# Softmax groups of one batch from batch 4 on, in an FFT filter with a soft mixture of experts

## The chip, the core and the metric

The kernel runs on one core of a Trainium2 chip. The metric is the device time of one launch in microseconds (us), the median of several runs. The layouts of inputs and outputs on the host are not timed.

## What is computed

x has 8 batches of 2496 rows and 256 columns. Each column is filtered in the frequency domain, and the filtered rows, all 19968 of them, go through a soft mixture of 8 experts with 4 slots each.

```python
y = irfft(rfft(x, axis=1) * (filt_r + 1j * filt_i), n=2496, axis=1)   # per batch
x = y.reshape(8 * 2496, 256)
logits = x @ phi                                   # (19968, 32)
d = exp(logits - logits.max(0)); d /= d.sum(0)     # softmax over all rows: dispatch
slot_input = d.T @ x                               # (32, 256), then each expert's MLP:
slot_out = relu(slot_input[e] @ w1[e]) @ w2[e]     # 4 slots for each e
c = exp(logits - logits.max(1)); c /= c.sum(1)     # softmax over the 32 slots: combine
out = c @ slot_out
```

The softmax over all rows is taken in groups of batches, with a running maximum and running sums, as in online softmax.

## The kernel before, in words

The inverse transform is never made for y: by linearity the logits and the slot inputs are formed from the filtered spectra, and only logits and weights are transformed.

A batch goes through these steps. `s1_unit(b, u)`, 11 for each batch, splits x into a high part `xh` (ScalarE, ACT) and a low part `xl` (GpSimd, POOL), multiplies both by a small DFT (three matmuls, L308), and writes the result `at` to DRAM. `x_unit(b, c)`, 10 for each batch, loads it in another order (`ash`), does the second DFT (L339), and multiplies by the filter on VectorE (DVE; L352, L353, L355) with help from POOL (L355, L356). `t_unit(b, c)`, 10 for each batch, transposes the product (L366) into a spectra tile `y_b_c`, copied out by ACT (L368); every second one also makes logits (`l`, L377, copied to `lt`). A spectra tile is kept until its group has used it, in `ypool`, a ring of `YB` buffers of 2 KB for each partition.

When the last batch of a group has its spectra, `chain(g)` runs. In order, by tile names: `ltr` (transposes of `lt`, copied by DVE to `lsb`), `v1` (L423, copied by ACT, L430), `v` (transposes, L443, copied by DVE), `lg` (logits in sequence order, L450; DVE takes maxima into `cm`, `cmax`), `mt` and `mb` (the maximum turned and spread, with `mx` and `dg` on DVE between them), `m_run` (the new running maximum, which needs that of the group before), `d` (subtract on DVE, exp on ACT, L489), `u` (L506, copied by ACT, L516), `u2` (transposes, L523, copied by DVE), `dt` (L537, copied by ACT), `dd` (transposes, L553, copied by DVE), `z` and `s` (L561, L581: the sums over the group's spectra tiles, which are free after it), and `s_run`, the running sum. The combine softmax of the same logits (`rm`, L602 to L610, exp L605) goes on beside it. A chain of a pair has 128 rows where one of a single batch has 64; the tiles `cc` (lsb, u2), `ca` (v1, u, dt) and `cb` (v, d, dd) have one buffer each, so a chain in the pool `work` begins when the one before has let go of them. The last chain has tiles of its own, in the pool `late`, and four PSUM banks; the others share two.

A chain is a generator; after each slot of the main loop the oldest one is moved on by two steps. The instructions so recorded are then put in order by a scheduler, which plans each engine's order by times of its own; on the chip each engine takes its instructions strictly in that order. What waits for what is therefore fixed when the program is built.

After the last batch the expert weights, 64 tiles of 256 KB on SyncE's (SP's) DMA queue, go into whatever is free: five tiles in `late`, then the oldest spectra buffers, then the buffers of the finished steps, and at the end the spectra buffers of the last two batches. Then come `psi`, the experts (`h` L816, `o` L833), and the output: for each batch in `OUT_ORDER`, matmuls (L903), copies into `ob` tiles of 1 MB (L912), and their DMAs.

The names that the change touches:

```python
GROUPS = ((0, 1), (2, 3), (4, 5), (6,), (7,))       # chain(g) for each
YB = 34                                             # buffers of spectra tiles
load_ws(ypool, "y", YB - 2 * CPB)                   # weights into the oldest 14 of them
obp_cm, obp = open_pool("obp", 6, "right")          # output tiles
```

Of the kernel before, what the change touches and what calls it, by code (L numbers as in the profile page):

```python
# [35 lines left out]
THIRDS = ((20, 0), (20, 1), (20, 2), (21, 0))  # L36
NE, SPE, FF = 8, 4, 1024
SLOTS = NE * SPE
GROUPS = ((0, 1), (2, 3), (4, 5), (6,), (7,))
NG = len(GROUPS)  # L40
NSPILL = 2
OUT_ORDER = (4, 5, 0, 1, 2, 3, 6, 7)
# [13 lines left out]
WM = 3  # L56
MV = 4
PA = 6
YB = 34
WL = 5  # L60
SB = 3

# [157 lines left out]
def fft_soft_moe(ctx, tc, x, fr, fi, fny, phi, w1, w2, cst, w1q, bmat, out):  # L220
# [35 lines left out]
    def open_pool(name, bufs, side):  # L256
        cm = tc.tile_pool(name=name, bufs=bufs, side=side, reuse_waits="tile")
        return cm, cm.__enter__()

    lgp_cm, lgp = open_pool("lgp", 1, "left")  # L260
    ypool_cm, ypool = open_pool("ypool", YB, "left")
    x0_cm, x0p = open_pool("x0p", 6, "left")
# [127 lines left out]
    def chain(g):  # L390
        bs = GROUPS[g]
        wk = late_pool[0] if g == NG - 1 else work
# [315 lines left out]
    assert next(ash_next, None) is None and next(b_next, None) is None  # L708
    last = {bs[-1]: g for g, bs in enumerate(GROUPS)}
    active = []  # L710
# [10 lines left out]
    def hop_slot(n):  # L721
        for _ in range(HOPS):
            hop()
# [18 lines left out]
    def load_ws(pool, tag, n, each=1, bufs=None):  # L742
        for _ in range(n):
            if len(wt) == len(order):
                return
            t = pool.tile([P, each * 512], F32, tag=tag, name=f"w_{len(wt)}", bufs=bufs)
            for k in range(min(each, len(order) - len(wt))):
                load_w(t[:, k * 512 : (k + 1) * 512])

    last_s1 = max(at_slot)  # L750
    for n in range(NS + LT):
# [25 lines left out]
        hop_slot(n)  # L777
    load_ws(ypool, "y", YB - 2 * CPB)
    load_ws(prod, "ash", ASH, bufs=ASH)
# [9 lines left out]

    load_ws(ypool, "y", YB)  # L790
    work_cm.__exit__(None, None, None)
    tail_cm, tail = open_pool("tail", 2, "left")
    for g in range(NSPILL):
        lgs[g] = tail.tile([KR, NH, len(GROUPS[g]), 2, SLOTS], F32, tag="cl", name=f"cl_{g}", bufs=NSPILL)
        sp.dma_start(lgs[g], c_dram[g])
# [52 lines left out]
    late_cm.__exit__(None, None, None)  # L848
    prod_cm.__exit__(None, None, None)
    tabs_cm.__exit__(None, None, None)  # L850
    obp_cm, obp = open_pool("obp", 6, "right")

    outs = [(ps_x, "x"), (ps_c, "c"), (ps_s1, "s1")]
    nout = [0]
    where = {b: (g, b2) for g, bs in enumerate(GROUPS) for b2, b in enumerate(bs)}

# [5 lines left out]
    def combine(b, st):  # L862

        g, b2 = where[b]
        nb = len(GROUPS[g])
        cl = lgs[g]
# [96 lines left out]
```

## Time and profile before

| what | value |
|---|---|
| median of 3 runs | 427.81 us (427.04 to 427.97) |
| profiled execution, whole | 425.78 us |
| its span, first to last instruction | 423.9 us |
| TensorE (PE) busy | 374.5 us, 88% |
| DVE, ACT, POOL busy | 269.8, 218.6, 201.9 us |
| moved by DMA | 107.07 MB, mean 253 GB/s |
| mean granted TensorE clock | 0.944 |

The durations below come from one profiled execution; 1.9 us of its time lie outside its span. Names in profile rows have lost their numbers and their digits: `s` on L308 is `s1`, `s` on L581 is the sum, `v` on L423 is `v1`, `u` on L523 is `u2`. Each fp32 matmul counts as two instructions on most lines. A row of the timeline has start, duration, engine and line; the distance from one row's start to the next is what a piece takes of PE, since matmuls overlap.

### The profile page before, as it was taken

What the parts mean: (1) busy time and instruction counts of PE and PEld (TensorE: products, weight loads), DVE (VectorE), ACT (ScalarE), POOL (GpSimd) and SP (SyncE); (2) the same over time, 40 slices, a digit from 0 to 9 for tenths busy, and PEclk for the clock granted to TensorE, in tenths of its full rate; (3) what the DMA queues carried; (4) which work ended last, traced back from release to release, by engine and by line L of the source; (5) the groups of instructions that cost most, each with busy time, mean ns of one, the idle gap of its engine ahead of it and who ended that gap; (6) DMA issues with size and microseconds to landing.
All of it is one profiled execution on the core that took longest, in us unless ns stands there. A gap on an engine that the chain in (4) does not pass through costs nothing.

```text
span 423.9 us, 12672 instructions
## 1 busy us (share of the span) xinstructions
PE 374.5 (88%) x5065; PEld 291.3 (69%) x5065; DVE 269.8 (64%) x496; ACT 218.6 (52%) x475; POOL 201.9 (48%) x234
## 2 busy tenths in 40 slices
PE   7557998999999999999989999989998799999740
PEld 2225876788877787886867688778767435898730
DVE  1341764886989955878998387896378322787330
ACT  2465666676677656765792333461446121675320
POOL 0027778797768655965966056572200401750000
PEclk9688999999999999999999999999998999999555
DMA  8999999999889686978996524333199895699994
GB/s 209 238 306 288 331 321 327 334 294 344 246 262 337 213 264 206 289 214 256 269 280 167 186 82 121 101 103 101 55 344 347 268 275 185 249 394 381 386 362 166
DMA packets 61820, 107.07 MB, mean 253 GB/s; under 512 B 6142, under 2 KB 37758, under 8 KB 60226
## 3 DMA queue, kind: packets, MB, share of 16 engines
q1 hardware_dynamic: 61762, 106.26, 79.3%
q8 instruction: 40, 0.66, 0.6%
q14 instruction: 18, 0.15, 0.1%
HBM read 63.50 MB, written 42.74 MB: 251 GB/s over the span
## 4 chain that ended last, share of the span: by engine, by line
PE 61%; DMA 16%; DVE 12%; ACT 3%; issue 2%; SPq 2%; POOL 0%; ACTq 0%; DVEq 0%
PE x L339 15%; PE s L308 8%; PE t L366 6%; DMA out<-obr 6%; DMA xt<-in_x 6%; PE s L581 4%; PE l L377 4%; PE out L903 3%; PE v L423 3%; PE dt L537 2%; DMA ash<-a_dram 2%; DVE t L353 2%; PE o L833 2%; PE lg L450 2%; PE s L305 2%
## 5 line engine op out<-in xcount | busy, mean ns | idle before, releaser
L295 POOL TENSOR_TENSOR xl<-xt,xh 117x512 fp32r<-117x512 f32 x77 | 103.0, 1350 | 52.7 <-ACT xh L294 49.9
L339 PE MATMUL x<-b_t,ash 128*128 128x128 f32 x640 | 91.5, 284 | 6.1 <-DMA ash<-a_dram 3.1
L339 PEld LDWEIGHTS x<-b_t,ash 128*128 128x128 f32 x640 | 81.2, 194 | 17.0 <-issue 5.0
L356 POOL TENSOR_TENSOR yt<-yt,t 128x256 f32<-128x256 f32 x80 | 65.9, 826 | 40.7 <-DVE t L353 30.5
L352 DVE TENSOR_TENSOR yt<-x,fr_t 128x512 f32<-128x512 f32 x80 | 54.7, 684 | 39.9 <-PE x L339 36.9
L294 ACT CAST xh<-xt 117x512 fp32r<-117x512 f32 x77 | 46.8, 622 | 35.4 <-DMA xt<-in_x 12.1
L368 ACT COPY y<-t 128x512 f32<-128x512 f32 x80 | 46.5, 591 | 34.3 <-PE t L366 28.6
L312 ACT COPY at<-s 120x512 f32<-120x512 f32 x83 | 48.4, 587 | 21.7 <-PE s L305 8.6
L353 DVE TENSOR_TENSOR t<-x,fi_t 128x512 f32<-128x512 f32 x80 | 54.3, 678 | 0.0
L366 PE MATMUL t<-cst_t,yt 128*128 128x128 f32 x320 | 48.5, 276 | 0.7 <-POOL yt L356 0.4
L355 DVE TENSOR_TENSOR yt<-yt,t 128x256 f32<-128x256 f32 x60 | 43.3, 730 | 0.8
L366 PEld LDWEIGHTS t<-cst_t,yt 128*128 128x128 f32 x320 | 37.3, 141 | 7.9 <-issue 3.1
L308 PE MATMUL s<-xh,w1h 117*120 117x512 f32 x77 | 36.0, 468 | 6.5 <-ACT xh L294 5.5
L903 PE MATMUL out<-so_h,st 32*128 32x256 f32 (+1 forms) x320 | 36.3, 329 | 3.3 <-ACT obr L912 2.4
L903 PE MATMUL out<-so_l,st 32*128 32x256 f32 (+1 forms) x320 | 34.4, 311 | 0.0
L903 PEld LDWEIGHTS out<-so_h,st 32*128 32x128 f32 (+1 forms) x320 | 29.9, 206 | 6.5 <-ACT obr L912 3.0
L308 PE MATMUL s<-xl,w1h 117*120 117x512 f32 x77 | 32.2, 419 | 0.3 <-POOL xl L295 0.2
L308 PE MATMUL s<-xh,w1l 117*120 117x512 f32 x77 | 31.1, 404 | 0.0
L355 POOL TENSOR_TENSOR yt<-yt,t 128x256 f32<-128x256 f32 x20 | 16.2, 811 | 30.5 <-DVE t L353 24.2
L903 PEld LDWEIGHTS out<-so_l,st 32*128 32x128 f32 (+1 forms) x320 | 30.3, 209 | 0.0
L377 PE MATMUL l<-yt,phi_t 128*32 128x128 f32 x640 | 26.1, 278 | 0.9 <-ACT y L368 0.7
L912 DVE COPY ob<-out 128x512 f32<-128x512 f32 x32 | 20.6, 684 | 7.6 <-PE out L903 7.3
(118 smaller groups left out, 552.6 us busy)
## 6 DMA issues: line engine op xcount, KB each, us to landing
ash<-a_dram SPq DMA_DIRECT2D x80, 256.0 KB
a_dram<-at SPq DMA_DIRECT2D x80, 240.0 KB
xt<-in_x SPq DMA_DIRECT2D x40, 448.0 KB
w<-in_w SPq DMA_DIRECT2D x64, 256.0 KB
out<-ob SPq DMA_DIRECT2D x12, 1024.0 KB
out<-ob SPq DMA_DIRECT2D x8, 512.0 KB
out<-obr SPq DMA_DIRECT2D x8, 448.0 KB
xt<-in_x SPq DMA_DIRECT2D x8, 224.0 KB
```

Source lines behind the costliest of these rows:

```text
L294: act.copy(xh, xs)
L295: pool_e.tensor_tensor(out=xl, in0=xs, in1=xh.bitcast(F32), op=ALU.subtract)
L308: pe.matmul(ps, w, xx, start=(n == 0), stop=(n == 2))
L312: act.copy(at, ps)
L339: pe.matmul(ps[:, 2 * k + dh].rearrange("q r c -> q (r c)"), ash[:, k, dh * P : (dh + 1) * P], b_t[:, t0 + k, :], start=True, stop=True,)
L352: dve.tensor_tensor(out=yt, in0=ps, in1=frv, op=ALU.mult)
L353: dve.tensor_tensor(out=t2, in0=ps[:, :, ::-1, :], in1=fiv, op=ALU.mult)
L355: add.tensor_tensor(out=yt[:, :, 1, :], in0=yt[:, :, 1, :], in1=t2[:, :, 1, :], op=ALU.add)
L356: pool_e.tensor_tensor(out=yt[:, :, 0, :], in0=yt[:, :, 0, :], in1=t2[:, :, 0, :], op=ALU.subtract)
L366: pe.transpose(pt[:, k, dh, :], yt[:, c % 2, 2 * k + dh].rearrange("q r c -> q (r c)"), ident)
L368: act.copy(y, pt.rearrange("k p h d -> k p (h d)"))
L903: nc.tensor.matmul(prs[k][0:rows, mm, :], st[q, n // 2, c0 : c0 + rows], (so_h, so_l)[n % 2][q, :], start=(n == 0), stop=(n == 3),)
```

## The change

Batches 4 and 5 no longer form a pair: chain 2 is batch 4 alone, chain 3 batch 5, chain 4 batch 6, chain 5 batch 7 (before: chain 2 batches 4 and 5, chain 3 batch 6, chain 4 batch 7). The ring of spectra tiles has 32 buffers for 34, and the output tiles have five buffers for six.

```diff
-GROUPS = ((0, 1), (2, 3), (4, 5), (6,), (7,))
+GROUPS = ((0, 1), (2, 3), (4,), (5,), (6,), (7,))
...
-YB = 34
+YB = 32
...
-    obp_cm, obp = open_pool("obp", 6, "right")
+    obp_cm, obp = open_pool("obp", 5, "right")
```

Since a scheduler sets the order, the change moves instructions in many places, from batch 3 on. Three of them matter below. A row has line, operation, tile written and tiles read (batch and unit in the first numbers of a name, or the group, then a running number), shape, and how often.

PE at the end of the main loop, from the last `x` unit on, before: the pair's `dt`, `dd` and `s` come right behind it.

```order
L339 MATMUL x_7_9_4569<-b_t_79,ash7_9_4338 128x128 x4
L523 MATMUL u2_2_8_4073<-cst_t_78,u_2_3881 128x128 x2
L537 MATMUL dt_2_0_4078<-cst_t_78,u2_2_4038 32x128
L537 MATMUL dt_2_0_4078<-b_t_79,u2_2_4038 32x128 x15
L537 MATMUL dt_2_4_4127<-b_t_79,u2_2_4038 32x128 x4
```

And now:

```order
L339 MATMUL x_7_9_4665<-b_t_79,ash7_9_4434 128x128 x4
L450 MATMUL lg_3_0_4110<-v_3_4061,cst_t_78 117x512
L450 MATMUL lg_3_8_4114<-v_3_4061,cst_t_78 117x192
L366 MATMUL t_7_7_4675<-cst_t_78,yt_7_6_4533 128x128 x4
L410 MATMUL ltr_7_0_4880<-cst_t_78,lt_7_4419 128x128
L377 MATMUL l_7_3_4682<-yt_7_6_4533,phi_t_81 32x128 x8
```

Behind the last `x` unit stood the end of the chain of batches 4 and 5; now batch 4's chain is done there, and batch 5's goes on from its `lg`.

PE behind the sums of batch 5, before: batch 6's chain starts among batch 7's last `t` and `l`.

```order
L581 MATMUL s_2_4209<-y_5_9_3574,dd_2_4155 32x256 x2
L410 MATMUL ltr_6_0_4362<-cst_t_78,lt_6_3731 128x128 x4
L377 MATMUL l_7_2_4493<-yt_7_4_4346,phi_t_81 32x128 x8
L366 MATMUL t_7_6_4534<-cst_t_78,yt_7_6_4437 128x128 x4
L410 MATMUL ltr_6_4_4368<-cst_t_78,lt_6_3731 128x128
```

And now:

```order
L581 MATMUL s_3_4354<-y_5_9_3763,dd_3_4332 32x256 x2
L410 MATMUL ltr_6_0_4458<-cst_t_78,lt_6_3894 128x128 x4
L410 MATMUL ltr_6_4_4464<-cst_t_78,lt_6_3894 128x128
L423 MATMUL v1_4_0_4495<-minv_t_277,lsb_4_4457 32x66 x14
L423 MATMUL v1_4_7_4511<-minv_t_277,lsb_4_4457 32x66 x14
```

Batch 6's chain starts at the same place of the program, behind batch 5's `s`, but nothing else is left to stand between its steps but batch 7's `u`, `u2`, `dt`, `dd` and `s`.

ACT while the first pair's sums are waited for, before: two tiles, `y_3_4` and `y_3_5`, are copied when buffers 0 and 1 of the 34 are free.

```order
L312 COPY at5_6_2385<-s1_5_6_2384 120x512
L368 COPY y_3_4_2214<-t_3_4_2209 128x512
L368 COPY y_3_5_2247<-t_3_5_2242 128x512
L384 COPY lt_3_2082<-l_3_2_2249 128x128
L368 COPY y_3_6_2288<-t_3_6_2283 128x512
```

And now:

```order
L312 COPY at5_9_2624<-s1_5_9_2623 120x512
L368 COPY y_3_2_2135<-t_3_2_2130 128x512
L368 COPY y_3_3_2174<-t_3_3_2169 128x512
L384 COPY lt_3_2083<-l_3_1_2176 128x128
L368 COPY y_3_4_2215<-t_3_4_2210 128x512
```

With 32 buffers the wait comes two tiles earlier, and three more `s1` units (`at5_7` to `at5_9`) stand before it.

## The prediction

> **What bounds the kernel now.** I read the page's slices first (busy tenths in 40 slices of 10.6 us, then granted clock and DMA), then busy time by stages, then PE's timeline at the end of the main loop.
>
> ```profile
> PE   7557998999999999999989999989998799999740
> PEclk9688999999999999999999999999998999999555
> DMA  8999999999889686978996524333199895699994
> ```
>
> PE is full from slice 6 to slice 35; DMA is the bound only at the start and from slice 36. The stages (start:end, length, then busy us of PE, PEld, DVE, ACT, POOL, then clock, DMA share, GB/s) are cut at the sums of batches 0 and 1, at those of 2 and 3, at the last `x` unit, at the sums of batches 4 and 5, at the `lg` of batch 6, at the sums of 6 and of 7, at the first output matmul, and where PE first waits for output buffers:
>
> ```profile
> 145.90:160.00 14.10, 14.10 (x181) 11.32 (x183) 9.01 (x14) 7.95 (x16) 8.83 (x9) 1.00 0.72 219
> 160.00:242.00 82.00, 78.98 (x1136) 62.01 (x1137) 61.82 (x99) 49.65 (x104) 50.82 (x45) 1.00 0.81 237
> 242.00:291.10 49.10, 46.88 (x780) 40.73 (x773) 41.90 (x75) 20.79 (x46) 28.11 (x38) 1.00 0.34 100
> 291.10:301.10 10.00, 9.27 (x191) 5.95 (x189) 2.43 (x6) 2.56 (x5) 0.69 (x1) 1.00 0.18 56
> 301.10:310.00 8.90, 8.90 (x196) 7.70 (x192) 5.41 (x10) 4.76 (x10) 2.79 (x4) 1.00 0.45 132
> 310.00:331.00 21.00, 19.23 (x358) 14.60 (x356) 15.18 (x48) 10.74 (x33) 0.00 (x0) 0.92 0.94 330
> 331.00:338.50 7.50, 5.32 (x107) 3.51 (x103) 3.05 (x10) 0.75 (x2) 4.79 (x12) 1.00 1.04 325
> 338.50:359.80 21.30, 20.05 (x223) 9.21 (x223) 4.87 (x9) 3.50 (x7) 1.04 (x2) 1.00 0.83 238
> 381.20:423.90 42.70, 23.22 (x327) 20.82 (x323) 15.03 (x28) 12.19 (x28) 0.00 (x0) 0.65 0.87 324
> ```
>
> Up to 291.1 us PE has work at nearly all times, so there the amount of PE work sets the time: 5.2 us of idle in 145.2. From 291.1 to 338.5 lie 47.4 us in which chains finish one behind the other; whatever is left over of batch 7 fills their gaps. So the question has two halves: when does the last `x` unit end, and how long is the stretch from there to the last sum.
>
> **The loop: work moved across its end, and work added.** PE's prices, from start to next start in the timeline:
>
> ```profile
> 213.45 1.89 PE L506 MATMUL u<-cst_t,d 117*32 117x60 f32 x128
> 257.87 0.60 PE L366 MATMUL t<-cst_t,yt 128*128 128x128 f32 x4
> 258.30 1.04 PE L443 MATMUL v<-cst_t,v 128*120 128x128 f32 x8
> 285.00 0.64 PE L377 MATMUL l<-yt,phi_t 128*32 128x128 f32 x16
> 285.58 2.05 PE L339 MATMUL x<-b_t,ash 128*128 128x128 f32 x16
> 287.47 1.04 PE L523 MATMUL u<-cst_t,u 128*128 128x128 f32 x8
> 296.63 4.52 PE L581 MATMUL s<-y,dd 128*32 128x256 f32 x80
> 310.02 1.12 PE L450 MATMUL lg<-v,cst_t 120*117 120x512 f32 x2
> 314.10 0.86 PE L443 MATMUL v<-cst_t,v 64*120 64x64 f32 x11 [0.39 <-ACT v L430]
> 319.64 0.27 PE L467 MATMUL mt<-cst_t,cmax 117*32 117x117 f32 x1
> 320.69 0.83 PE L523 MATMUL u<-cst_t,u 64*128 64x64 f32 x10 [0.77 <-ACT u L516]
> 321.45 0.40 PE L474 MATMUL mb<-dg,ones 32*128 32x32 f32 x2
> 328.69 2.35 PE L581 MATMUL s<-y,dd 128*32 128x256 f32 x40
> 332.60 1.18 PE L537 MATMUL dt<-b_t,u 128*32 128x128 f32 x35
> 334.52 0.77 PE L553 MATMUL dd<-cst_t,dt 128*128 128x128 f32 x5 [0.74 <-ACT dt L544]
> 336.04 2.35 PE L581 MATMUL s<-y,dd 128*32 128x256 f32 x40
> ```
>
> A `t` unit takes 0.43 us (257.87 to 258.30), an `l` 0.58, an `x` unit 0.95 (two rows' worth 285.58 to 287.47), a single batch's `s` 2.3. Two singles instead of a pair add 11 `v` transposes, 10 of `u2`, one `lg`, one `mt` and one `mb`, each small: about 0.3 + 0.3 + 0.3 + 0.7 = 1.6 us of PE in all. DVE gains some 3 us (`cmax`, `mx`, `dg`, `m_run`, `al`, `s_run` once more), ACT some 4 us (three `v1` and six `u` copies); in the loop both lie beside PE (ACT is busy 20.79 of 49.10 us), in the last chains they are counted below. If that cover is gone, the 3 us of DVE are what it costs.
>
> Before the last `x` unit now stands, and did not: batch 4's `dt`, `dd`, `z`, `s` (1.4 + 0.6 + 0.1 + 2.3 = 4.4 us; the `dt` row shows 35 of 40 instructions), one `l` and one `t` (1.0), a share of the extra `v` (0.3). Behind it now stands what was before it: batch 5's half of `lg` (1.1), of `u` (1.3, 88 of the 128 instructions in 1.89 us) and of `u2` (0.2). Net +3.1 us. Idle time: the wait for a spectra buffer now comes two tiles earlier in batch 3, so nine `s1` units run in the stretch where there were six, with PE work of 13 us in place of 14.1. POOL must make a low part for each:
>
> ```profile
> L295 POOL TENSOR_TENSOR xl<-xt,xh 117x512 fp32r<-117x512 f32 x77 | 103.0, 1350 | 52.7 <-ACT xh L294 49.9
> a_dram<-at SPq DMA_DIRECT2D x80, 240.0 KB
> ```
>
> 9 x 1.35 = 12.2 us, just under 13; DMA moves 480 KB for each unit, 4.3 MB, which takes this stretch to some 330 GB/s, what the stage from 310.0 us has. I take no added wait, at most +4 us: at the 237 GB/s of the next stage the 4.3 MB would take 18.2 us, 4.1 more than the stretch has. On the other side the 5.2 us of idle could shrink where the pair's long DVE pieces block `x` units:
>
> ```profile
> L488 DVE TENSOR_TENSOR d<-lg,m_run 117x512 f32<-117x512 f32 x2 | 2.9, 1490 | 0.0
> ```
>
> Those of batches 2 and 3 stay, those of 4 and 5 are halved; the stage of the latter has 2.2 us idle, of which I take none. Last `x` unit: 291.1 + 3.1 = 294.2, between 291 (2.2 us of idle and 1 of the work less) and 298.3.
>
> **From the last `x` unit to the last sum: three chains where there were two.** Rows for the steps (by form, 301 to 339 us: count | busy us, mean ns | idle before):
>
> ```profile
> L516 ACT COPY u<-u 64x240 f32<-64x240 f32 x8 | 2.4, 354 | 1.4 <-PE u L506 1.4
> L430 ACT COPY v<-v 64x462 f32<-64x462 f32 x4 | 2.3, 580 | 1.9 <-PE v L423 1.9
> L605 ACT ACTIVATE lg<-lg 117x352 f32<-117x352 f32 x4 | 1.9, 502 | 0.0
> L489 ACT ACTIVATE d<-d 117x256 f32<-117x256 f32 x4 | 1.5, 417 | 4.6 <-DVE d L488 4.6
> L602 DVE TENSOR_REDUCE rm<-lg 117x11 f32<-117x352 f32 x4 | 2.0, 509 | 0.0
> L411 DVE COPY lsb<-ltr 128x512 f32<-128x512 f32 x2 | 1.4, 691 | 2.4 <-PE ltr L410 2.4
> ```
>
> First leg, from the last `x` unit to the end of batch 5's sums. Before, 10.0 us (the pair's `dt`, `dd`, `s` were ready). Now it starts at batch 5's `lg`; before, batch 6's chain took 21.0 us over the same steps (310.0 to 331.0), with another chain in its gaps as now. Stepping through the new order with the rows' durations I come to 20.6. +10.6; bounds 17 and 22.
>
> Second leg, to the end of batch 6's sums. Before, 29.9 us, with batch 7's `t`, `l` and first steps among it. Now the chain has PE to itself. `ltr` to the end of the first `lg`: 0.5, a copy (0.69) behind `s_run`, three `v1` copies in series on ACT (0.58 each), `v` 0.8, a copy, 0.9: 5.9 with handovers. Maxima to `m_run`, past two `rm` (0.51 each) and batch 7's `mt`: 3.4. Then ACT's queue, which has batch 6's exp (3 x 0.4), its combine exp (2 x 0.5), batch 7's exp, two `u` copies, batch 7's combine exp (2 x 0.5, waiting for DVE) and only then the other four `u` copies: 7.4. `u2`, copy, `dt`, copy, `dd`, copies, `s`: 7.4. Sum 24.1, -5.8; bounds 21 and 28.
>
> Third leg, to the end of batch 7's sums: its `u2` is done before batch 6's `s`, so `dt` 1.4, copy 0.6, `dd` 0.5, copies 0.9, `z`, `s` 2.3 make 5.8 with handovers, where it was 7.4: -1.6; bounds 5 and 7.4.
>
> In all 50.5 us for 47.4: +3.1. The last sum ends at 294.2 + 50.5 = 344.7, where it ended at 338.5.
>
> **Weights and output.** The weights loaded at the end wait for spectra buffers and then for `h`:
>
> ```profile
> 336.73 14.98 SPq L736 DMA_DIRECT2D w<-in_w  x14
> 356.10 1.97 PE L833 MATMUL o<-w,ht 128*32 128x256 f32 x26
> ```
>
> Two buffers fewer put 16 loads there for 14, two of 262 KB at the 238 GB/s of that stage: 2.2 us. The last issue before is at 351.7, the last group of `o` starts at 356.1, and the loads start 5.8 for 7.4 us ahead of the last sum. I take 0.2 us, bounds 0 and 2. The ten loads that wait for batch 5's spectra come later but well ahead of `h`. The output stage is DMA's (324 GB/s with the drain at its end, PE 23.22 of 42.70 us busy): four output tiles of 1 MB in flight are still over 10 us of writing, so the fifth buffer instead of a sixth costs 0; bounds 0 and +1. The combine of batch 5 reads another logits tile, at the same cost.
>
> Sum: +3.1 + 3.1 + 0.2 = +6.4 us. The profiled execution, 425.78 with a span of 423.9, would be 432.2; it stands 2.0 below the median, so the median becomes 434.2.
>
> **Rivals.** One: `s1` runs dry in batch 3 (the +4 above), because DMA and POOL both sit at their limit there: 438.2. For it: 12.2 of 13 us; against it, xh, xl and output tiles are several deep.
>
> Two: the clock. In the last chains it fell once (0.92 in the stage from 310.0) though no PE wait there exceeded 0.8 us. In my stepping through the new order PE waits 3 us for ACT's queue ahead of batch 6's `u2`. The matmuls on the path of the second and third leg (two `dt`, `dd` and `s`, the rest once) sum to about 14.5 us; a third of them at half clock makes +5, half of them +7. I take +5: 439.2. The Trainium skill (TensorE: Matmul & The Clock Gate, Part 1) says that the gate falls to half rate after an idle window of about 3.4 us and opens after as long a busy one. By that rule a 3 us wait is on the edge of it; the trace before shows a drop without any such wait, so the rule alone does not decide.
>
> Three, faster: the pair's long DVE pieces were what left PE idle between 160 and 291.1 us (3.0 + 2.2 us), and with halves PE has none: -5.2 + 3.1 = -2.1 for the loop. It ends faster if the three legs then take under 49.5 us, which needs the first leg at 19.6 or less; with the tail as long as before, 427.8 - 2.1 = 425.7. Against it: most of that idle lies in batches 2 and 3, whose pair stays.
>
> Four: loop and tail cancel, for instance the first leg at 17 and the idle down by 2.5: 427.8.
>
> **Chances and range.** The forecast 0.58 (its own range 431 to 438), rival one 0.12, two 0.13, three 0.10, four 0.07. A measurement of this kernel can tell about 0.2%, 0.9 us, from no change. Faster 0.10, same 0.07, slower 0.83. The range takes in the rivals one and two, and on the low side the bounds of loop and first leg together (-3.2 and -3.6 from 434.2): 427.4 to 439.8.
>
> **What would show it.** On PE the last L339 near 294 us; three L581 groups of 40 instructions behind it, ending near 315, 339 and 345, with a wait for ACT's `u` (L516) ahead of batch 6's `u2`; L804 (`psi`) near 345.3; the span from there to the end as before, 85 us. ACT's wait of L368 for PE `s` L581 stays near 160 us with more L308 units ahead of it. I am wrong if the last L339 ends by 290 (idle bounded the loop), or if the first leg is under 17 us (the chain was stretched by what stood in its gaps, not by its own steps).

## The result and the profile after

The changed kernel takes 440.81 us (median of 4 runs, 439.47 to 445.33), the kernel before on the same chip 427.89 (427.04 to 429.06): ratio 1.035, 95% interval 1.0296 to 1.0403. (Ratios, here and below, leave out executions more than 1.5% above the fastest of the same kernel.) The forecast was 434.2 with a range to 439.8. The direction was right, the size was less than half of what came.

The changed kernel's profiled execution took 440.32 us, with a span of 438.5. Its slices (busy tenths, granted clock, DMA):

```profile
PE   8676988999998999999999999999869899999940
PEclk9679999999999999999999999999997999999555
DMA  8999999999799798977665243427760698499995
```

DMA now has a hole: the 31st slice (329 to 340 us) is 0, just ahead of the weights' load. The stages of the changed kernel, in the columns that the prediction explained, cut at the first sum, the last `x` unit, the sums of batches 5, 6 and 7, and the first output matmul:

```profile
147.40:160.40 13.00, 13.00 (x153) 9.65 (x151) 3.98 (x9) 9.48 (x18) 10.58 (x9) 1.00 0.88 265
160.40:297.40 137.00, 134.62 (x1965) 110.05 (x1965) 104.57 (x185) 71.52 (x156) 74.57 (x83) 1.00 0.59 177
297.40:317.70 20.30, 17.70 (x342) 13.01 (x340) 13.11 (x35) 9.16 (x26) 2.79 (x4) 1.00 0.77 261
317.70:343.20 25.50, 20.89 (x406) 17.09 (x407) 14.89 (x48) 10.28 (x31) 0.00 (x0) 0.87 0.29 99
343.20:348.80 5.60, 4.33 (x97) 2.65 (x85) 2.19 (x7) 0.75 (x2) 4.74 (x12) 1.00 0.88 278
348.80:374.70 25.90, 24.05 (x227) 10.11 (x227) 4.98 (x10) 3.50 (x7) 1.14 (x2) 1.00 0.88 252
374.70:438.50 63.80, 45.73 (x689) 40.95 (x689) 32.47 (x64) 26.67 (x62) 13.45 (x35) 0.74 0.86 322
```

The two stages of the kernel before that the prediction did not show cut this way:

```profile
160.00:291.10 131.10, 125.86 (x1912) 102.74 (x1910) 103.72 (x174) 70.44 (x150) 78.93 (x83) 1.00 0.63 186
359.80:423.90 64.10, 44.49 (x689) 39.80 (x689) 32.58 (x65) 26.69 (x62) 13.58 (x35) 0.77 0.86 320
```

The spans differ by 14.6 us: 0.4 up to the first sum, 5.9 from there to the last `x` unit (PE work +8.8, idle from 5.2 to 2.4), 4.0 in the three legs (51.4 for 47.4), 4.6 from the last sum to the first output matmul (25.9 for 21.3), -0.3 in the output stage. The medians differ by 12.9: the profiled execution of before stood 2.1 us under its median, the one of after 0.5 us.

**The loop.** PE's time from start to next start (idle included), from the first sum to the last `x` unit, grouped by what the forecast had as terms:

```
                                 before   after   change   forecast
s, dt, dd, z                      14.09   18.14    +4.05    +4.4
t, l, x and s1                    92.27   92.49    +0.22    +1.0
ltr, lg, v, u2, mt, mb            12.99   12.55    -0.44    -1.0
u (L506)                           6.62    5.95    -0.67    -1.3
v1 (L423)                          5.28    7.88    +2.60     0
sum                              131.25  137.01    +5.76    +3.1
```

Part of these rows is waiting. Without the waits that the timeline lists in them (4.8 us before, 2.2 after) PE's work changed by +4.2, +2.0, -0.4, 0.0 and +2.6 us, 8.3 in all: `u` did not get shorter (5.51 and 5.48 us). The second row grew because units moved across the first sum too: behind it now stand 42 `x` units, 43 `t` and 22 `l`, where there were 40, 40 and 20, and about three `s1` units fewer.

The largest gap is `v1`, the next is `u`. PE's timeline of the changed kernel shows batch 4's and batch 5's `v1` and batch 4's `u`:

```profile
241.56 1.00 PE L423 MATMUL v<-minv_t,lsb 128*32 128x66 f32 x28
244.74 1.69 PE L423 MATMUL v<-minv_t,lsb 128*32 128x66 f32 x52
264.16 1.88 PE L506 MATMUL u<-cst_t,d 117*32 117x60 f32 x64
267.01 0.87 PE L506 MATMUL u<-cst_t,d 117*32 117x60 f32 x24
286.69 1.00 PE L423 MATMUL v<-minv_t,lsb 128*32 128x66 f32 x28
290.10 1.69 PE L423 MATMUL v<-minv_t,lsb 128*32 128x66 f32 x52
```

(Times of `v1` and `u` matmuls are from here on the sums of the rows' durations; from start to next start they are a little less, 2.55 us for a single's `v1` and 2.70 for the pair's, as the expectations below have them.) 80 `v1` matmuls of a single take 2.69 us; the pair's 160 in the kernel before take 3.10 (four rows, shown with the second experiment). 64 `u` matmuls of a single take 1.88 us; the prediction's row has 128 of a pair in 1.89. Half the instructions, nearly the same time. Both write 32 columns of the array at `q = (b2 * 2 + h) * 32` or `(b2 * 2 + th) * 32`: a pair goes round four column groups, a single round two. The experiments test whether that is the reason.

**The weights.** What the `o` matmuls (L833) waited for, before (first block) and after:

```profile
L833 PE MATMUL o<-w,ht x128: 379/379/403, 349.0 to 357.7; 128*32 128x256 f32 x128
  issue: 0.7, 3
  DMA w<-in_w: 0.3, 1
```

```profile
L833 PE MATMUL o<-w,ht x128: 376/379/403, 359.4 to 372.5; 128*32 128x256 f32 x128
  DMA w<-in_w: 3.9, 7
  issue: 0.9, 4
```

They start 10.6 us behind the last sum in both, but take 13.1 us in place of 8.7. SP's queue and its longest wait, and the end of the chain, in the changed kernel:

```profile
316.02 4.62 SPq L734 DMA_DIRECT2D w<-in_w  x10
341.58 5.95 SPq L736 DMA_DIRECT2D w<-in_w  x10
347.58 0.92 SPq L795 DMA_DIRECT2D cl<-c_dram  x2
348.97 17.50 SPq L736 DMA_DIRECT2D w<-in_w  x16
```

```profile
SPq L736 <- PE s L581: 20.9, 1, 20.9
```

```profile
343.09 4.99 DMA w<-in_w
348.17 11.70 DMA cl<-c_dram
359.94 6.10 DMA w<-in_w
366.11 5.68 DMA w<-in_w
```

SP stands 20.9 us behind the sums of batch 6. Then 26 loads of 262 KB and two logits tiles, some 8.1 MB, go in one burst from 341.6 on, and the last lands at 371.8: 30 us, 270 GB/s. The long wait is not what is new: before, SP waited 4.2 us for the same sums, and then 24 loads and the two logits tiles went behind them (10 from 329.37 us on, 14 from 336.73), at 287 GB/s up to 356. PE's `o` ends as soon as the last weight is there.

### The profile page after: what moved, and what is told of

It reads as the page before. It is cut to its first block, busy times and chain, and to the rows that moved or that the text cites. A ratio compares the mean times of both kernels' runs of the same rounds, so it can differ in the third digit from the quotient of the medians.

```text
span 438.5 us, 12788 instructions
## 1 busy us (share of the span) xinstructions
PE 389.8 (89%) x5091; PEld 300.0 (68%) x5091; DVE 269.7 (62%) x520; ACT 222.2 (51%) x492; POOL 198.0 (45%) x234
## 4 chain that ended last, share of the span: by engine, by line
PE 58%; DMA 21%; DVE 8%; ACT 4%; POOL 2%; issue 2%; SPq 1%; DVEq 0%; POOLq 0%; ACTq 0%
PE x L339 14%; PE s L308 8%; PE t L366 7%; PE out L903 6%; DMA xt<-in_x 5%; PE l L377 4%; DMA w<-in_w 4%; PE s L581 3%; PE v L423 3%; DMA out<-obr 3%; DMA a_dram<-at 3%; DMA cl<-c_dram 3%; PE u L506 3%; DMA ash<-a_dram 3%; PE lg L450 2%
## 5 line engine op out<-in xcount | busy, mean ns | idle before, releaser
L295 POOL TENSOR_TENSOR xl<-xt,xh 117x512 fp32r<-117x512 f32 x77 | 100.6, 1319 | 55.6 <-ACT xh L294 54.4
L339 PE MATMUL x<-b_t,ash 128*128 128x128 f32 x640 | 88.8, 280 | 4.8 <-DMA ash<-a_dram 4.6
L339 PEld LDWEIGHTS x<-b_t,ash 128*128 128x128 f32 x640 | 79.5, 191 | 15.3 <-issue 6.4
L356 POOL TENSOR_TENSOR yt<-yt,t 128x256 f32<-128x256 f32 x80 | 65.2, 816 | 44.3 <-DVE t L353 35.1
L903 PE MATMUL out<-so_h,st 32*128 32x256 f32 (+1 forms) x320 | 37.5, 334 | 1.6 <-ACT ob L912 0.6
L903 PE MATMUL out<-so_l,st 32*128 32x256 f32 (+1 forms) x320 | 35.5, 315 | 0.0
L871 POOL TENSOR_TENSOR c<-lg,r_all 117x352 f32<-117x352 f32 x8 | 6.1, 786 | 45.1 <-PE s L581 43.1
```

Of the source, the lines that this page charges most:

```text
L295: pool_e.tensor_tensor(out=xl, in0=xs, in1=xh.bitcast(F32), op=ALU.subtract)
L339: pe.matmul(ps[:, 2 * k + dh].rearrange("q r c -> q (r c)"), ash[:, k, dh * P : (dh + 1) * P], b_t[:, t0 + k, :], start=True, stop=True,)
L356: pool_e.tensor_tensor(out=yt[:, :, 0, :], in0=yt[:, :, 0, :], in1=t2[:, :, 0, :], op=ALU.subtract)
L903: nc.tensor.matmul(prs[k][0:rows, mm, :], st[q, n // 2, c0 : c0 + rows], (so_h, so_l)[n % 2][q, :], start=(n == 0), stop=(n == 3),)
```

## The experiments

Times here are against the kernel before on the same chip (medians 427.78, 427.64 and 426.76 us in the three sets of runs). Single executions of one kernel lie several us apart, above all in the stages up to the first sum and from the first output matmul on, where DMA is the bound. So I compare stages too: from the first sum to the last `x` unit (131.2 us in the kernel before, 137.0 in the changed one), from there to the last sum (47.1 and 51.3), and `o` (9.1 and 13.5, ends included). The changed kernel was not run again in these sets, so a difference from its 440.81 us is one between sets of runs.

**Single batches packed into four column groups**, in the changed kernel:

```diff
-  q = (b2 * 2 + h) * 32                                   # v1
+  q = (b2 * 2 + h) * 32 + (64 * ((t - t0) % 2) if nb == 1 else 0)
   ...
+  for o in range(2):      # nb == 1: two copies in place of one
+      act.copy(v1[0:R, :, :, t0 + o : t0 + n : 2], pv[64 * o : 64 * o + 64, o:n:2]...)
-  q = (b2 * 2 + th) * 32                                  # u
+  q = ((b2 if nb == 2 else h) * 2 + th) * 32
   ...
+  p0 = 0 if nb == 2 else 64 * h                           # u's copy reads from p0 on
```

> The changed kernel, but in the chains of single batches the v1 matmuls take turns between column groups 0-63 and 64-127 (by the tile's parity), and the u matmuls put the second half of the pieces into column groups 64-127; a single then uses four 32-column groups as a pair does. Same instructions on PE, one more copy on ACT for each of the three v1 tiles. Theory one (narrow matmuls in two of the four column groups take PE as long as a pair's in four, so each single pays a pair's v1 and u): 80 v1 in about 1.4 us instead of 2.55 and 88 u in about 1.5 instead of 2.6; the last x unit comes 3.0 to 3.7 us earlier, the last legs 1 to 2 us shorter, 4 to 6 us in all (435 to 437). Theory two (v1 and u are slow in a single because of its waits, for copies and exponentials): PE's rows for v1 and u stay above 2.2 us each and the time is within 1 us of the changed kernel's 440.8, or above it by the added copies.

It took 437.59 us (433.44 to 438.02), ratio 1.0228 (1.0155 to 1.0301), where the changed kernel had 1.035. The stage to the last `x` unit took 134.3 us, 2.7 less than 137.0, the three legs 50.1, 1.2 less. The groups of PE, all batches, of the changed kernel and then of this one:

```profile
L506 PE MATMUL u<-cst_t,d 117*32 117x60 f32 (+1 forms) x704 | 19.0, 227 | 1.8 <-ACT u L516 1.1 <-ACT d L489 0.5
L423 PE MATMUL v<-minv_t,lsb 128*32 128x66 f32 x640 | 16.6, 222 | 0.6 <-DVE lsb L411 0.6
```

```profile
L513 PE MATMUL u<-cst_t,d 117*32 117x60 f32 (+1 forms) x704 | 16.4, 230 | 4.2 <-ACT u L524 1.7 <-ACT d L496 1.2 <-issue 1.2
L423 PE MATMUL v<-minv_t,lsb 128*32 128x66 f32 x640 | 12.6, 223 | 1.1 <-DVE lsb L411 0.6 <-ACT v L434 0.5
```

The count and the mean length of one matmul are the same; PE is busy 4.0 us less for `v1` and 2.6 less for `u`, because they overlap more. Batch 4's `v1` in this run:

```profile
241.46 0.66 PE L423 MATMUL v<-minv_t,lsb 128*32 128x66 f32 x28
244.29 1.00 PE L423 MATMUL v<-minv_t,lsb 128*32 128x66 f32 x52
```

1.66 us in place of 2.69. Theory one holds for the loop: what is left there is 3.1 us over before (134.3 for 131.2), as much as the forecast had, though not from the forecast's terms alone (see the point on idle below). The gain is 3.2 us between the medians, under the 4 to 6 expected, and 5.2 by the two ratios, so the time does not fix its size; the stages give 2.7 + 1.2, and `o` still takes 13.1 us (13.5 before the packing, ends included), as the runs without the last weight loads explain. The 1.2 us of the legs did not come where `v1` stands on the path: the second leg took 26.0 us for 25.5, with six copies of `v1` on ACT, 2.50 us, in place of three. The third took 4.0 for 5.6.

**The groups not taken in turn**, in the kernel before, for the `v1` of batches 4 and 5 alone:

```diff
+  turns = [(t, b2, h) for t in range(t0, t0 + n) for b2 in range(nb) for h in range(2)]
+  if g == 2:
+      turns.sort(key=lambda x: x[1:])
```

> The kernel before, with one change: the 160 v1 matmuls of the pair of batches 4 and 5 are issued column group by column group (seven in a run into the same 32 columns) and not in turn over the four groups. Same instructions, same tiles, same count. Theory one (matmuls of 32 columns run beside each other when they stand next to each other in different column groups; a single batch has half the groups, so its matmuls take twice as long each): a run in one group has no partner, so the 160 matmuls that took 2.7 us take about 160 x 64 ns = 10 us (a single's 80 in two groups took 2.55 us, 32 ns each; with one group twice that), the last x unit comes about 7 us later, and the time is about 434 to 435. Theory two (each matmul costs what its issue costs, and a single's are slow for other reasons): v1 stays at 2.7 us and the time within 1 us of before.

432.2 us (429.27 to 438.56), ratio 1.0104 (1.006 to 1.0148). PE's timeline, the pair's `v1` in the kernel before and then here (the profiled execution was the one of 438.56 us; the granted clock from 249 to 262 us is 1.00 in it):

```profile
250.28 0.55 PE L423 MATMUL v<-minv_t,lsb 128*32 128x66 f32 x24
251.35 0.67 PE L423 MATMUL v<-minv_t,lsb 128*32 128x66 f32 x32
253.69 1.01 PE L423 MATMUL v<-minv_t,lsb 128*32 128x66 f32 x56
254.96 0.87 PE L423 MATMUL v<-minv_t,lsb 128*32 128x66 f32 x48
```

```profile
250.23 0.99 PE L424 MATMUL v<-minv_t,lsb 128*32 128x66 f32 x16
251.74 2.09 PE L424 MATMUL v<-minv_t,lsb 128*32 128x66 f32 x40
255.06 2.81 PE L424 MATMUL v<-minv_t,lsb 128*32 128x66 f32 x56
258.63 2.32 PE L424 MATMUL v<-minv_t,lsb 128*32 128x66 f32 x48
```

3.10 us became 8.21 for the same 160 matmuls: 51 ns each instead of 19, where a single's two groups give 34 (2.69 us for 80). The time followed by 4.4 us (2.6 to 6.3 by the interval); the estimate of 64 ns was too high. Theory two would have left both as they were. So neighbours in different column groups overlap, and that is what a single loses. Each matmul has a weight load of its own, and the loads follow the same pattern (12.6 us busy for 640 of them in the kernel before, 17.7 here, 110 ns each in both), so these runs don't tell whether it is the loads or the matmuls that take their time one after the other within a group.

The Trainium skill (TensorEngine Tiling (Array Packing), Tiling Modes and Theoretical Speedup) says that column tiles work independently and gives up to 4 times for 32 columns; here four groups in turn gave 2.6 times over runs in one group.

**The same packing in the kernel before**, whose singles are batches 6 and 7 (the diff is the one above).

> The kernel before with the same packing of v1 and u in its two singles (batches 6 and 7). Theory one (two column groups cost what four do): its v1 and u get shorter by 1 us each for each batch, but most of that lies in the last chains, beside waits: 1 to 3 us faster than before (425 to 427). Theory two (waits, not groups): within 0.9 us of before, or slower by the added copies on ACT.

429.7 us, ratio 1.0016 (0.9965 to 1.0067): no change that can be told. Its `v1` falls from 14.4 to 12.6 us of busy PE and its `u` from 15.3 to 14.3, but the legs take 47.3 us for 47.1. The 1 to 3 us that I expected did not come. There PE waits for the chain's other engines, and the added copies on ACT work against the packing: batch 7's `v1` is copied in 2.46 us for 1.61, and PE waits 1.20 us for it where it waited 0.39. The two are not parted by this run.

**Without the last 16 weight loads**, in the changed kernel and in the kernel before:

```diff
   def load_w(t):
       ...
+  if order[len(wt)][:2] == ("w2", 1):      # in load_ws
+      for key in order[len(wt):]:
+          wt[key] = wt[("w2", 0) + key[2:]]
+      return
```

> The changed kernel without the last 16 weight loads (experts 4 to 7 use the second weights of experts 0 to 3, so this part of the result is another). Theory one (the o stage waits 3.9 us for weights that land last in one burst, because the loads sit behind batch 5's sums in SP's queue): the o matmuls run without that wait, 8.7 us as before instead of 13.1, and the time falls by about 4.4 us, to 436.4. Theory two (the burst delays nothing, the wait is that of the output's other inputs, which come as late): within 1 us of 440.8.

> The kernel before without the same 16 weight loads (as in the run above this leaves out part of the experts' weights). Both theories: the o stage waits 0.3 us for weights in the kernel before, so the time stays within 0.9 us of before, or falls by up to 1 us. A fall as large as in the changed kernel (over 3 us) would say that leaving out the bytes helps by itself, and theory one would have no support from the other run.

(The sums that the loads wait for are batch 6's, not batch 5's: SP's wait of 20.9 us ends at 341.6, during batch 6's `s`.) The changed kernel went to 437.04 us (436.12 to 438.14), ratio 1.0238 (1.0173 to 1.0303), 3.8 less than with all loads; the kernel before to 428.07, ratio 1.0015 (0.9976 to 1.0054). The `o` matmuls of the changed kernel without these loads:

```profile
L837 PE MATMUL o<-w,ht x128: 379/379/403, 359.8 to 368.5; 128*32 128x256 f32 x128
```

8.7 us, as before the change, with no wait for DMA left. So the 4.4 us are the wait for the last loads of the burst, and in the kernel before, the same loads cost nothing that can be told.

**Both together**: packed, and without the 16 loads.

> The changed kernel with the packed v1 and u and without the last 16 weight loads (this leaves out part of the experts' weights). If the two causes stand side by side they add: 437.6 with the packing, less 4.4 for the wait of the o stage, 433 to 434; what is left over the kernel before is then 5 to 6 us, the two terms of the forecast that had nothing to do with them (loop 3.1, last chains 3.1). If they are one and the same delay seen twice, the time stays near 436 to 437.

432.81 us (429.41 to 435.13), ratio 1.0122 (1.0054 to 1.0189); last `x` unit 134.0 us behind the first sum, legs 49.6, `o` 9.0. The two causes add. What is left over before, 5.2 us, is close to the 6.2 that the forecast had for loop and legs; how far that is luck, the points on idle and legs below say.

**The smaller ring alone**: `YB = 32` in the kernel before.

> The kernel before with 32 spectra buffers in place of 34, all else as it was. What the smaller ring costs by itself. The forecast had 0.2 us for the weights and nothing for the loop. Reading after the result: the o stage waits already 0.3 us for weights before, so there is no slack, and two more loads of 262 KB behind the sums cost up to 2 us there: 428 to 430. Rival (the ring of 32 stalls the loop, and this, not the packing, is what moved the last x unit): the last x unit 3 us or more later than before, counted from the first sum, and 431 or more.

429.46 us, ratio 1.0029 (0.999 to 1.0068): too small to tell by time, but its `o` shows the wait:

```profile
L833 PE MATMUL o<-w,ht x128: 379/379/403, 350.6 to 361.4; 128*32 128x256 f32 x128
  DMA w<-in_w: 2.2, 5
```

2.2 us in place of 0.3, and the last sum comes 179.8 us behind the first in place of 178.4. This run's order puts the last `x` unit behind batch 6's first transposes, so the stage to that unit can't be compared; by the last sum the rival of 3 us and more is out.

**The fifth output buffer given back**: the changed kernel with six.

> The changed kernel with six output buffers as before in place of five. The forecast had 0 for the fifth buffer, and the stage from the first output matmul took 63.8 us against 64.0: within 1 us of the changed kernel's 440.8. Rival (output tiles run out with five): 1 us or more faster, and a shorter last stage.

441.94 us (440.51 to 446.27), and 65.6 us from the first output matmul to the end in place of 63.8. So nothing shows that five buffers cost time.

**The opposite step**: batches 6 and 7 as a fourth pair, with all loads and without the last 16.

```diff
-GROUPS = ((0, 1), (2, 3), (4, 5), (6,), (7,))
+GROUPS = ((0, 1), (2, 3), (4, 5), (6, 7))
```

> The opposite step: the kernel before with batches 6 and 7 as a fourth pair (four pairs, no single). Theory one: PE has less to do (the two singles' v1 and u cost 5 us more than a pair's, the small steps 1.6 us), but the pair's chain starts only behind batch 7's last l (near 306 us) and takes some 30 us, so the last sum ends near 336, 2 us earlier than before; and all 20 spectra of the last two batches come free only then, so some 34 weight loads and the logits stand behind it, 10.2 MB at about 300 GB/s, 34 us: the o stage ends near 370 in place of 358, and the time is 435 to 440. Rival (the weights do not set the end of the o stage, PE does): the time falls with the last sum, 423 to 427.

> The same four pairs without the last 16 weight loads (this leaves out part of the experts' weights). Theory one: 16 loads of 262 KB less behind the last sum, 4.2 MB at 300 GB/s, 14 us: the o stage waits no more or little, and the time is 10 to 12 us below that of the kernel with all loads, near the kernel before or up to 2 us under it. Rival (the weights do not set the end): the same time as with all loads.

With all loads 425.98 us, ratio 0.9995 (0.9949 to 1.0041): as before, and my expectation was wrong. PE's `v1` and `u` cost 12.2 and 13.1 us (14.4 and 15.3 before), but the last sum ends at 338.8, 338.4 before: the pair's longer chain takes up what PE saves. Nor do 34 loads stand behind it:

```profile
326.62 1.03 SPq L795 DMA_DIRECT2D cl<-c_dram  x2
334.24 17.64 SPq L736 DMA_DIRECT2D w<-in_w  x24
```

The logits are loaded ahead of the sums and 24 weights from 334.2 on, 7.4 us earlier than in the changed kernel; `o` waits 0.2 us. I had miscounted the loads, so this run does not decide on the weights. The version without 16 loads gave runs from 422.3 to 993 us; nothing can be read from it.

## Why the prediction was wrong, point by point

- **Loop, +3.1: measured +5.9.** The steps that failed are "two singles instead of a pair add ... about 1.6 us of PE in all", which left out `v1` (+2.6), and batch 5's half of `u` as "1.3, 88 of the 128 instructions in 1.89 us", which priced a single's matmul like a pair's (-0.7 measured for -1.3, and 0.0 without the waits in the row). Both took time to go with the number of instructions; it goes with the number of turns over the column groups. The trace of before had the prices of a single:

```profile
305.03 1.67 PE L423 MATMUL v<-minv_t,lsb 128*32 128x66 f32 x52
316.94 2.77 PE L506 MATMUL u<-cst_t,d 117*32 117x60 f32 x88
```

  The pair's `v1` took 0.87 us for 48 (at 254.96), and its `u` 1.89 for 128. Moved work of `s`, `dt`, `dd` and `z`, 4.4 forecast, was right (4.05, or 4.2 without the waits).
- **Idle: none gained, by the forecast.** PE's idle in this stretch fell from 5.2 to 2.4 us, and the extra matmul work hid it. Where batches 4 and 5 had their pair's chain, 2.2 us went to none (57.70 us busy of the 57.70 from 239.7 us on); where batches 2 and 3 have theirs, 3.0 became 2.4. So idle went away with the pair, as rival three has it, at half its size. That DVE's long pieces had made it is not shown: of those 2.2 us one wait, 0.59, was for DVE, and the largest, 1.11 in `u`, ended in nothing that the profile shows. That the loop came to the forecast's +3.1 once the packing was restored is partly luck: PE was busy 131.92 us of the 134.3, 6.1 more than before, and the idle that went away took off 2.9.
- **`s1` in batch 3: no added wait.** Right: 13.00 us with PE busy throughout, DMA share 0.88, POOL 10.58 us; rival one did not come.
- **Legs: 20.6, 24.1 and 5.8 us forecast, 20.3, 25.5 and 5.6 measured.** Stepping through the order came close. Of the second leg's 1.4 us more, 1.2 lie in its first step, `ltr` to the end of the first `lg`, 7.1 us for 5.9: the forecast let ACT's three copies of `v1` set the pace there (1.74 us), but PE needed 2.6 us for `v1` itself, at a granted clock of 1.00. So a single's `v1` cost more than the forecast gave it here too. Maxima to `m_run` took 3.8 for 3.4, ACT's queue up to `u2` 7.0 for 7.4, the rest 7.6 for 7.4. PE in this leg:

```profile
319.09 2.58 PE L423 MATMUL v<-minv_t,lsb 128*32 128x66 f32 x80 [0.41 <-DVE lsb L411]
329.66 6.09 PE L506 MATMUL u<-cst_t,d 117*32 117x60 f32 x134
335.68 0.83 PE L523 MATMUL u<-cst_t,u 64*128 64x64 f32 x10
```

  Rival two's lower clock came, 0.63 in the middle of the leg,

```profile
325.00:334.00 9.00, 6.35 (x96) 5.52 (x95) 8.22 (x31) 5.06 (x16) 0.00 (x0) 0.63 0.04 12
```

  behind PE waits of 1.1 and 1.0 us, none near 3, but most of its price did not. The wait of 3 us ahead of batch 6's `u2` did not show because PE was then at work on 134 `u` matmuls at the lower clock; ACT's last four copies for this `u2` (1.07 us from 334.14 on) ended at 335.2, 0.5 us before it began, so ACT's queue would have held it until about then anyway. What the clock cost in the smaller pieces, no run here separates. The Trainium skill (TensorE: Matmul & The Clock Gate, Part 1) names an idle window of about 3.4 us; here the drop came with several short waits, as it did before the change.
- **Weights, +0.2 with bounds 0 and 2: measured +4.4.** The step that failed is the slack, which I took from the last issue (351.7) to the last `o` (356.1). The load still had to land, and `o` waited 0.3 us for it already: the slack was zero. Then both of the forecast's own small numbers became a delay, two loads more (2.2 us, the wait that the smaller ring alone showed) and a third leg shorter by 1.8 us, since the burst starts with the sums of batch 6 and not with those of batch 7. From the former to the end of `o` it was 27.1 us before and 29.7 now. This split is read from single executions: with the same loads as now, the packed kernel took 27.7 us there and the one with six output buffers 28.6, so it is argued, not shown. That the wait for the last loads is the 4.4 us is shown.
- **Output buffers, 0.** Right, as far as the run with six shows.
- **Two sums.** By the forecast's own numbers rival four (first leg 3.6 less, idle 2.5 less) comes to 428.1, not 427.8; and nothing is worked out for the range's upper end of 439.8, 0.6 above rival two.

## What to carry to other kernels

A matmul that fills 32 of 128 columns costs by what stands next to it: before you split a group that was made to fill the column groups, look how long its half takes on PE, not how many instructions it has. Slack of a load is counted to its landing and from the event that starts the burst, and an engine that already waits 0.3 us for it has none. Work saved on PE counted where PE had no idle; in the last chains of the kernel before, 3 us less of it, bought with more copies on ACT, changed nothing.

## What was not expected of the hardware

The same 160 matmuls of 32 columns took 3.10 us in turn over four column groups and 8.21 us in runs of one group, though a single record shows 222 ns in either (the mean of all 640): the records' lengths don't tell the cost, the distance between starts does (2.70 and 7.93 us). And a logits tile of 643.5 KB stood in the chain for 11.7 us amid loads of 262 KB that stood for 5 to 6; the whole burst ran at 270 GB/s, where the output stage moves 322.
